# A diffusion-transformer block on one core: x of image 0 in two loads, x*s + x for the first scaling, the scale rows in two parts, another order of the head

## The chip, the cores and the metric

The kernel runs on 1 core of one Trainium2 chip. A core has five engines with a queue of instructions each: TensorE (PE; its weight loads are listed as PEld), VectorE (DVE), ScalarE (ACT), GpSimd (POOL) and SyncE (SP). An engine works through its queue in order and waits on semaphores that other engines, or landed DMAs, raise. DMAs are issued from the queues of SP, ACT and POOL and are moved by 16 DMA engines. The metric is device microseconds of one execution.

## The reference

Two images (B = 2) of N = 256 tokens and D = 1152 features go through one transformer block whose normalised inputs are scaled and shifted by a condition vector c. All data are bfloat16.

```python
mod = (_silu(c) @ w_mod).reshape(B, 6, 1, D)
shift_a, scale_a, gate_a, shift_m, scale_m, gate_m = [mod[:, i] for i in range(6)]
h = _layernorm(x, axis=-1) * (1 + scale_a) + shift_a
qkv = (h @ wqkv).reshape(B, N, 3, H, Dh)          # H = 2 heads, Dh = 576
attn = _softmax(einsum('bqhd,bkhd->bhqk', q, k) * Dh ** (-0.5), axis=-1)
a = einsum('bhqk,bkhd->bqhd', attn, v).reshape(B, N, D) @ wo
x = x + gate_a * a
h2 = _layernorm(x, axis=-1) * (1 + scale_m) + shift_m
return x + gate_m * (_gelu(h2 @ w_fc1) @ w_fc2)   # w_fc1: 1152 x 4608
```

Only the first three lines and the K part of the fourth matter for the change: silu(c), the rows scale_a of w_mod, the layer norm of x, its scaling, and K = h @ (K columns of wqkv). The shift of h is not needed for K here: it adds the same amount to every score of a query, which softmax cancels, so K is made from the scaled input alone ("HK").

## The kernel before

**Planner and queues.** The kernel is written as units of work (`S.unit`, `S.op`), each with an engine, an estimated duration and the regions it reads and writes. From the regions the planner derives the waits. Units of PE and of SP keep the order in which the text gives them. ACT, DVE and POOL are ordered by a list schedule from the estimated durations, except that `S.first` (L940) writes out the order of the head of DVE's and ACT's queues by hand. An engine waits in its queue for whatever the next instruction needs, whatever stands behind it. For a function of ACT the compiler puts the load of the function table ahead of the first instruction that uses it. Where an instruction needs more than one wait, all but the last stand as instructions of their own ahead of it.

**Tiles.** Each image has two token tiles of 128 tokens: tiles t = 0, 1 are image 0, tiles 2, 3 image 1. The feature dimension is cut in nine groups of 128 (kt = 0 to 8). KC = 5 is where the scale columns are cut: groups 0 to 4 are made first, by small matmuls that leave them along partitions ("sca_0" to "sca_8", one for each of nine contraction steps, L849 to L857); groups 5 to 8 come later as rows of two ("scb", L879, 36 matmuls, four for each contraction step).

**Loads (L699 to L713).** ACT issues two: "touch" (L699, 128 pieces of 64 B out of rows spread over w_mod; nothing reads them) and "ld_c" (c). SP issues x of image 0 in one load (`dma(X[:, 0:2, :], xv[0], ...)`, L701, 4608 bytes a partition), x of tile 2 ("ld_x2"), the scale columns of groups 0 to 4 in four loads ("ld_sc0_0" to "ld_sc0_8"), K's weights wk0 and wk1, x of tile 3 ("ld_x3"), wk2 to wk4, the scale columns of groups 5 to 8 in three loads ("ld_sc5_0", "ld_sc5_3", "ld_sc5_6"), wk5 to wk8, and so on.

**The head.** PE first runs matmuls on dummy data ("warm"). It turns c with a transpose ("c_T"). DVE halves it ("c_half", L732), ACT takes tanh ("c_tanh", L733), DVE finishes silu ("c_silu", L734). The statistics of even tiles run on ACT (`ln_stats_act`, L747: a pass of squares "sq", a pass for the mean "sum"; DVE then makes the variance in two small steps, "nvar" and "veps"), those of odd tiles on DVE (`ln_stats_dve`, L738: three "bn", "aggr", "veps"). POOL raises the variance to the power -1/2 ("rstd"). DVE normalises ("xn_t", L763). PE transposes the tile ("xnT_t", L773). For image 0, group 0 is copied from PSUM ("xnT_cp0_0"), 1 is added to the scale columns ("sc1a_0", L807), and each group is multiplied by its column of 1 + s ("hk_kt_b", L812; b is the image). K is then accumulated group by group: `k_pair` (L831) makes two output tiles of 256 columns, and "hk_0_0" opens the first of them.

**Around scb.** After K of image 1's first pair of output tiles (groups 0 to 4, `k_pair((0, 2, 1, 4, 3), 0, 1)`, L878), PE runs the 36 matmuls of scb, and DVE transposes the result ("scb_T", L884), adds 1 ("sc1a_5", L886) and scales groups 5 to 8 of both images, while PE goes on with two more pairs of image 1 for groups 0 to 4. Groups 5 to 8 of K follow. Behind them PE makes the shift rows ("sh"), Q, the scores, V, the output projection and the two MLP matmuls.

Of the kernel before, what the change touches and what calls it, by code (L numbers as in the profile page):

```python
# [493 lines left out]
ALU = mybir.AluOpType  # L494
# [3 lines left out]
P = 128  # L498
NTOK = 512
D = 1152  # L500
KT = 9
# [3 lines left out]
EPS = 1e-5  # L505
# [4 lines left out]
KC = 5  # L510
# [33 lines left out]
def build_kernel(nc, x, c, wqkv, wo, w_mod, w_fc1, w_fc2, out):  # L544
    S = Sched()
# [4 lines left out]
    with (  # L550
# [147 lines left out]

        dma(sb(O_PT, 64)[0:128, :], w_mod.rearrange("(p k) f -> p k f", k=9)[:, 0, D:D + 32], 128 * 64, "touch", eng="act")  # L699
        dma(CSB[0:18, :], c.rearrange("b (k p) -> (b k) p", p=P), 18 * 256, "ld_c", eng="act")  # L700
        dma(X[:, 0:2, :], xv[0], 2 * P * D * 2, "ld_x0")  # L701
        dma(X[:, 2, :], xv[1][:, 0, :], P * D * 2, "ld_x2", run=2304)
        for (ka, kb, cuts) in ((0, KC, (0, 2, 5, 8, 9)), (KC, KT, (0, 3, 6, 9))):
            w = (kb - ka) * P
            for k0, k1 in zip(cuts, cuts[1:]):
                dma(WSC[:, k0:k1, ka * P:kb * P], wmod_v[:, k0:k1, D + ka * P:D + kb * P], (k1 - k0) * P * w * 2,
                    "ld_sc%d_%d" % (ka, k0), run=w * 2)
            for kt in range(ka, kb):
                dma(WK[:, kt, :], wqkv_v[:, kt, D:2 * D], P * D * 2, "ld_wk%d" % kt, run=2304)
                if kt == 1:  # L710
                    dma(X[:, 3, :], xv[1][:, 1, :], P * D * 2, "ld_x3", run=2304)
# [13 lines left out]
        dve(600, lambda e: e.memset(Q4B, 0.0), [], [Q4B], "zq4b")  # L725
        for i in range(7):
            S.unit("pe", 430.0, "warm_a%d" % i)
            mm(ps32(7), IDENT, Q4B, True, True)
# [18 lines left out]
        def ln_stats_act(src, junk, mv_t, msq, rstd_t, tag):  # L747
            mean, var = mv_t[:, 0:1], mv_t[:, 1:2]
            act(1420, lambda e: e.activation(out=junk, in_=src, func=ACTF.Square, scale=D ** -0.5, accum_out=msq), [src], [junk, msq], "sq_" + tag)
            act(1420, lambda e: e.activation(out=junk, in_=src, func=ACTF.Identity, scale=1.0 / D, accum_out=mean), [src], [junk, mean], "sum_" + tag)  # L750
            dve(170, lambda e: e.scalar_tensor_tensor(out=var, in0=mean, scalar=mean, in1=msq, op0=ALU.mult, op1=ALU.subtract),
                [mean, msq], [var], "nvar_" + tag)
            dve(150, lambda e: e.tensor_scalar(out=var, in0=var, scalar1=-1.0, scalar2=EPS, op0=ALU.mult, op1=ALU.add), [var], [var], "veps_" + tag)
            pool(650, lambda e: e.tensor_tensor(out=rstd_t, in0=var, in1=NHALF, op=ALU.pow), [var, NHALF], [rstd_t], "rstd_" + tag)
# [57 lines left out]
        def hk(kt, b, eng="dve"):  # L812
# [3 lines left out]
            if eng == "act":  # L816
# [3 lines left out]
                [src, s1], [dst], "hk_%d_%d" % (kt, b))  # L820

        def k_mm(kts, j, b, bank, half):

# [22 lines left out]

        warm(5, "b")
        for kt in range(0, 2):
            mod_kt(WSC, kt, 0, "sca_%d" % kt, (0, KC))  # L849
        warm(4, "c")  # L850
        xn_T(1)
        for kt in range(2, 5):
            mod_kt(WSC, kt, 0, "sca_%d" % kt, (0, KC))
        xn_T(0)
        warm(2, "d")
        for kt in range(5, 9):
            mod_kt(WSC, kt, 0, "sca_%d" % kt, (0, KC))  # L857
        warm(1, "e")
        xn_T_copy(0, (0,), "dve")
        sc1a(0, KC)  # L860
        for kt in range(KC):
            hk(kt, 0, "act" if kt == 4 else "dve")
        xn_T_copy(0, (8,), "act")
# [14 lines left out]
        k_pair((0, 2, 1, 4, 3), 0, 1)  # L878
        S.unit("pe", KT * 4 * 27.0, "scb")  # L879
        for kt in range(KT):  # L880
            quad_mm(7, WSC[:, kt, :], KC, KT, kt)
        n = 32 * (KT - KC)
        sct, scr = ps32(7, 0, n), MT[:, 0:n]
        dve(c_dve_psum32(n), lambda e: e.transpose(scr, sct), [sct], [scr], "scb_T")  # L884
        scv, sco = scr.rearrange("p (k r) -> p k r", r=32)[:, :, 0:2], SC1A.rearrange("p (k b) -> p k b", b=2)[:, KC:KT, :]
        dve(170, lambda e: e.tensor_scalar(out=sco, in0=scv, scalar1=1.0, scalar2=None, op0=ALU.add), [scv], [sco], "sc1a_%d" % KC)  # L886
        for kt in range(KC, KT):
            for b in range(2):
                hk(kt, b)
        k_pair((0, 2, 1, 4, 3), 1, 1)  # L890
        k_pair((0, 2, 1, 4, 3), 2, 1)
# [34 lines left out]
        for kt in range(KT):  # L926
            for b in range(2):
# [5 lines left out]
                else:  # L933
# [6 lines left out]
        S.first = {  # L940
            "dve": ["zq4b", "bn_ln1_1_0", "c_half", "bn_ln1_1_1", "bn_ln1_1_2", "c_silu", "aggr_ln1_1", "veps_ln1_1", "nvar_ln1_0", "veps_ln1_0",
                    "xn_1", "xn_0", "nvar_ln1_2", "veps_ln1_2", "xnT_cp0_0", "sc1a_0", "hk_0_0", "hk_1_0", "hk_2_0", "hk_3_0", "xn_2",
                    "bn_ln1_3_0", "bn_ln1_3_1", "bn_ln1_3_2", "aggr_ln1_3", "veps_ln1_3", "xn_3", "hk_0_1", "hk_2_1", "hk_4_1", "xnT_cp1_6", "scb_T", "sc1a_5"],
            "act": ["touch", "ld_c", "sq_ln1_0", "c_tanh", "sum_ln1_0", "sq_ln1_2", "sum_ln1_2", "xnT_cp0_8", "xnT_cp0_5", "hk_4_0",
                    "hk_1_1", "hk_3_1", "xnT_cp1_8", "xnT_cp1_5"],
# [362 lines left out]
```

## Time and profile before

| what | us |
|---|---|
| median of 3 runs (244.64 to 244.94) | 244.71 |
| the profiled execution | 245.13 |
| its span | 243.4 |
| PE busy in the span | 237.7 (98%) |
| DVE busy | 116.1 (48%) |
| ACT busy | 67.0 (28%) |
| POOL busy | 22.4 (9%) |
| mean DMA rate over the span | 212 GB/s |

Busy times of a view are sums over instructions; in a timeline each line gives the start in us from the span's beginning, the duration, the engine (a q behind it is its queue: issues and waits), the line of the kernel, the operation, what it writes and reads, how many such instructions the line merges, and in brackets the idle time of the engine before it with what ended that. The profiled execution is one execution; it took 0.42 us more than the median of the runs. Landings of single DMAs are times from the span's start as the trace records them.

### The profile page before, as it was taken

What the parts mean: (1) busy time and instruction counts of PE and PEld (TensorE: products, weight loads), DVE (VectorE), ACT (ScalarE), POOL (GpSimd) and SP (SyncE); (2) the same over time, 40 slices, a digit from 0 to 9 for tenths busy, and PEclk for the clock granted to TensorE, in tenths of its full rate; (3) what the DMA queues carried; (4) which work ended last, traced back from release to release, by engine and by line L of the source; (5) the groups of instructions that cost most, each with busy time, mean ns of one, the idle gap of its engine ahead of it and who ended that gap; (6) DMA issues with size and microseconds to landing.
All of it is one profiled execution on the core that took longest, in us unless ns stands there. A gap on an engine that the chain in (4) does not pass through costs nothing.

```text
span 243.4 us, 3964 instructions
## 1 busy us (share of the span) xinstructions
PE 237.7 (98%) x1700; PEld 145.3 (60%) x1700; DVE 116.1 (48%) x227; ACT 67.0 (28%) x138; POOL 22.4 (9%) x40
## 2 busy tenths in 40 slices
PE   6998999999999999999999999999999999999995
PEld 2587844466667666888644444444556565666664
DVE  2663357888982589769999700000022222111112
ACT  4820340436514206983223332222000000000000
POOL 1300000000023186400000110000000000000000
DMA  6999999999995999969953589100000000000000
GB/s 221 368 375 391 389 386 387 403 413 406 392 350 150 352 389 391 391 201 402 352 166 91 177 294 375 59 0 3 0 16 19 16 16 16 19 16 16 19 28 20
DMA packets 30299, 51.58 MB, mean 212 GB/s; under 512 B 1611, under 2 KB 16971, under 8 KB 30283
## 3 DMA queue, kind: packets, MB, share of 16 engines
q1 hardware_dynamic: 29600, 50.14, 57.6%
q0 software_dynamic: 512, 1.19, 1.5%
q8 instruction: 13, 0.21, 0.4%
q10 hardware_dynamic: 171, 0.01, 0.0%
q14 instruction: 3, 0.02, 0.0%
HBM read 50.15 MB, written 1.19 MB: 211 GB/s over the span
## 4 chain that ended last, share of the span: by engine, by line
PE 91%; DMA 5%; SPq 3%; issue 0%; DVE 0%
PE psum L693 90%; DMA arena<-in_w_mod_dram 5%; SPq L674 3%; PE psum L696 1%; DVE arena L1250 0%; DVE arena L1251 0%
## 5 line engine op out<-in xcount | busy, mean ns | idle before, releaser
L693 PE MATMUL psum<-arena 128*128 128x384 bf16 (+8 forms) x1611 | 234.4, 314 | 2.9 <-POOL arena L719 1.5
L693 PEld LDWEIGHTS psum<-arena 128*128 128x128 bf16 (+2 forms) x1611 | 140.0, 97 | 92.8 <-issue 4.1
L1250 DVE TENSOR_TENSOR arena<-psum,arena 128x384 f32<-128x384 f32 (+2 forms) x13 | 6.9, 527 | 88.8 <-PE psum L693 88.8
L1163 ACT ACTIVATE arena<-psum 128x512 bf16<-128x512 f32 (+1 forms) x45 | 22.8, 511 | 42.4 <-PE psum L693 42.4
L688 ACT ACTIVATE arena<-psum 128x512 bf16<-128x512 f32 (+6 forms) x37 | 18.7, 534 | 36.9 <-PE psum L693 36.6
L1063 DVE SCALAR_TENSOR_TENSOR arena<-arena 128x1152 f32<-128x1152 bf16 x16 | 21.4, 1418 | 0.0
L1034 DVE SCALAR_TENSOR_TENSOR arena<-arena 128x896 f32<-128x896 bf16 x16 | 17.7, 1145 | 0.0
L690 DVE CAST arena<-psum 128x512 bf16<-128x512 f32 (+1 forms) x12 | 7.7, 647 | 11.1 <-PE psum L693 11.0
L674 POOL DMA_DIRECT2D dit_scratch<-arena x6 | 3.6, 605 | 93.6 <-ACT arena L688 54.3
L1129 POOL TENSOR_TENSOR arena<-arena 128x384 f32<-128x384 f32 x12 | 10.9, 912 | 11.2 <-DVE arena L1128 9.1
L741 DVE BATCH_NORM_STATS2 arena<-arena 128x6 f32<-128x384 f32 (+1 forms) x18 | 9.5, 551 | 4.2 <-DMA arena<-in_x_dram 3.5
L1134 ACT ACTIVATE arena<-arena 128x1152 bf16<-128x1152 f32 x4 | 5.4, 1344 | 9.5 <-DVE arena L1133 9.5
L1128 DVE TENSOR_TENSOR arena<-psum,arena 128x384 f32<-128x384 f32 x12 | 6.5, 549 | 2.9 <-PE psum L693 2.8
L696 PE MATMUL psum<-arena 128*128 128x128 bf16 (+1 forms) x89 | 7.1, 219 | 0.4 <-DMA arena<-in_c_dram 0.4
L696 PEld LDWEIGHTS psum<-arena 128*128 128x128 bf16 (+1 forms) x89 | 5.8, 98 | 2.7 <-DMA arena<-in_c_dram 1.3
L1251 DVE TENSOR_TENSOR arena<-arena 128x384 bf16<-128x384 f32 (+2 forms) x13 | 6.9, 527 | 0.5
L1153 ACT ACTIVATE arena<-psum,arena 128x128 bf16<-128x128 bf16 x16 | 6.1, 454 | 3.0 <-PE psum L696 2.2
L1150 DVE TENSOR_SCALAR arena<-psum,arena 128x128 bf16<-128x128 bf16 x20 | 5.5, 338 | 2.9 <-PE psum L696 2.9
L978 ACT ACTIVATE arena<-psum,arena 128x256 bf16<-128x256 f32 x8 | 3.7, 470 | 0.4 <-DVE arena L975 0.3
L745 POOL TENSOR_TENSOR arena<-arena 128x1 f32<-128x1 f32 x6 | 3.3, 553 | 4.8 <-DVE arena L744 4.8
L931 ACT ACTIVATE arena<-arena 128x256 bf16<-128x256 bf16 x6 | 2.5, 494 | 3.3 <-DVE arena L925 3.3
L974 DVE TENSOR_REDUCE arena<-psum 128x2 f32<-128x512 f32 x4 | 2.8, 688 | 0.9 <-PE psum L693 0.9
(57 smaller groups left out, 52.5 us busy)
## 6 DMA issues: line engine op xcount, KB each, us to landing
arena<-in_w_fc_dram SPq DMA_DIRECT2D x9, 1152.0 KB, 7.3
arena<-in_w_fc_dram SPq DMA_DIRECT2D x4, 2592.0 KB, 18.1
arena<-in_w_mod_dram SPq DMA_DIRECT2D x3, 1920.0 KB, 19.6
arena<-in_wqkv_dram SPq DMA_DIRECT2D x18, 288.0 KB, 10.2
arena<-in_w_mod_dram SPq DMA_DIRECT2D x3, 864.0 KB, 13.1
arena<-in_wqkv_dram SPq DMA_DIRECT2D x1, 2592.0 KB, 16.5
arena<-in_wo_dram SPq DMA_DIRECT2D x1, 2592.0 KB, 26.0
arena<-in_w_mod_dram SPq DMA_DIRECT2D x1, 2592.0 KB, 17.9
```

Source lines behind the costliest of these rows:

```text
L674: return S.op(eng, 500.0 if eng == "sp" else 150.0, lambda e: e.dma_start(dst, src), reads=[src], writes=[dst], name=name, dma_bytes=nbyte ...
L688: act(c_act(n), lambda e: e.activation(out=dst, in_=src, func=ACTF.Copy), [src], [dst], name)
L690: dve(c_dve_psum16(n) if psum16 else c_dve_psum32(n), lambda e: e.tensor_copy(dst, src), [src], [dst], name)
L693: S.instr(lambda e: e.matmul(o, lhsT=l, rhs=r, start=st, stop=sp, **kw), reads=[l, r], writes=[o])
L696: S.instr(lambda e: e.transpose(o, i_, idn), reads=[i_, idn], writes=[o])
L741: dve(550, lambda e, s=s, o=o: e.bn_stats(out=o, in_=s), [s], [o], "bn_%s_%d" % (tag, ci))
L1034: dve(150 + FG * 1.1, lambda e, o=o, w=w, s1=s1: e.scalar_tensor_tensor(out=o, in0=w, scalar=s1, in1=o, op0=ALU.mult, op1=ALU.add), [w, s1 ...
L1063: u = dve(1300, lambda e, o=o, w=w, s1=s1: e.scalar_tensor_tensor(out=o, in0=w, scalar=s1, in1=o, op0=ALU.mult, op1=ALU.add), [w, s1, o], ...
L1129: S.op("pool", 930, lambda e, xs=xs, x1c=x1c: e.tensor_tensor(out=x1c, in0=x1c, in1=xs, op=ALU.add), reads=[x1c, xs], writes=[x1c], name=" ...
L1163: act(c_act(ntok), lambda e: e.activation(out=dst, in_=o, func=ACTF.Gelu_apprx_tanh), [o], [dst], "gelu_%d_%d" % (f, tok0))
L1250: dve(c_dve_psum32(w), lambda e, o=o, gm=gm, t1=t1: e.tensor_tensor(out=t1, in0=o, in1=gm, op=ALU.mult), [o, gm], [t1], "fc2_t1_%d_%d" % ( ...
L1251: dve(c_dve_32(w), lambda e, t1=t1, x1c=x1c, ost=ost: e.tensor_tensor(out=ost, in0=t1, in1=x1c, op=ALU.add), [t1, x1c], [ost], "fc2_out_%d ...
```

## The change

It changes six things, all before the shift rows:

1. The load "touch" is taken out, so ld_c is the first on ACT's queue.
2. x of image 0 is loaded in two halves, one for each tile; x of tile 3 is loaded one place earlier, ahead of wk1.
3. The numbers and places of the warm matmuls change (7, 5, 4, 2, 1 become 4, 8, 3, 1, 2), and both transposes xnT_0 and xnT_1 stand side by side, tile 0 first.
4. For group 0 of image 0, and for group 5 of both images, the scaling is done as x*s + x with the raw s ("hk_raw"), ahead of the step that adds 1.
5. scb is cut in two: contraction steps 0 to 5, then six K matmuls, then steps 6 to 8.
6. The order of the head of DVE's and ACT's queues changes: DVE does c_half and c_silu first and xn_0 before xn_1; ACT does c_tanh before sq_0, and takes hk_3_0 over from DVE. In `ln_stats_act`, eps is added to the mean square before the variance is made rather than after.

```diff
-        dma(sb(O_PT, 64)[0:128, :], w_mod.rearrange("(p k) f -> p k f", k=9)[:, 0, D:D + 32], 128 * 64, "touch", eng="act")
         dma(CSB[0:18, :], c.rearrange("b (k p) -> (b k) p", p=P), 18 * 256, "ld_c", eng="act")
-        dma(X[:, 0:2, :], xv[0], 2 * P * D * 2, "ld_x0")
+        for t in range(2):
+            dma(X[:, t, :], xv[0][:, t, :], P * D * 2, "ld_x%d" % t, run=2304)
...
-                if kt == 1:
+                if kt == 0:
                     dma(X[:, 3, :], xv[1][:, 1, :], P * D * 2, "ld_x3", run=2304)
...
-        for i in range(7):
+        for i in range(4):
             S.unit("pe", 430.0, "warm_a%d" % i)
...
-            dve(170, lambda e: e.scalar_tensor_tensor(out=var, in0=mean, scalar=mean, in1=msq, op0=ALU.mult, op1=ALU.subtract),
+            dve(150, lambda e: e.tensor_scalar(out=msq, in0=msq, scalar1=EPS, scalar2=None, op0=ALU.add), [msq], [msq], "veps_" + tag)
+            dve(170, lambda e: e.scalar_tensor_tensor(out=var, in0=mean, scalar=mean, in1=msq, op0=ALU.mult, op1=ALU.subtract, reverse1=True),
                 [mean, msq], [var], "nvar_" + tag)
-            dve(150, lambda e: e.tensor_scalar(out=var, in0=var, scalar1=-1.0, scalar2=EPS, op0=ALU.mult, op1=ALU.add), [var], [var], "veps_" + tag)
...
+        def hk_raw(kt, b, sc):
+            dst, src = HK[:, kt, b * 256:(b + 1) * 256], HX[:, kt, b * 256:(b + 1) * 256]
+            dve(330, lambda e: e.scalar_tensor_tensor(out=dst, in0=src, scalar=sc, in1=src, op0=ALU.mult, op1=ALU.add),
+                [src, sc], [dst], "hk_%d_%d" % (kt, b))
...
-        warm(5, "b")
+        warm(8, "b")
         for kt in range(0, 2):
             mod_kt(WSC, kt, 0, "sca_%d" % kt, (0, KC))
-        warm(4, "c")
+        warm(3, "c")
+        xn_T(0)
         xn_T(1)
         for kt in range(2, 5):
             mod_kt(WSC, kt, 0, "sca_%d" % kt, (0, KC))
-        xn_T(0)
-        warm(2, "d")
+        warm(1, "d")
         for kt in range(5, 9):
             mod_kt(WSC, kt, 0, "sca_%d" % kt, (0, KC))
-        warm(1, "e")
+        warm(2, "e")
         xn_T_copy(0, (0,), "dve")
+        hk_raw(0, 0, ps32(7, 0, 1))
         sc1a(0, KC)
-        for kt in range(KC):
-            hk(kt, 0, "act" if kt == 4 else "dve")
+        for kt in range(1, KC):
+            hk(kt, 0, "act" if kt >= 3 else "dve")
...
-        S.unit("pe", KT * 4 * 27.0, "scb")
-        for kt in range(KT):
+        S.unit("pe", 6 * 4 * 27.0, "scb_0")
+        for kt in range(6):
+            quad_mm(7, WSC[:, kt, :], KC, KT, kt)
+        k_pair((0, 2, 1), 1, 1)
+        S.unit("pe", 3 * 4 * 27.0, "scb_1")
+        for kt in range(6, KT):
             quad_mm(7, WSC[:, kt, :], KC, KT, kt)
...
+        for b in range(2):
+            hk_raw(KC, b, scv[:, 0, b:b + 1])
         dve(170, lambda e: e.tensor_scalar(out=sco, in0=scv, scalar1=1.0, scalar2=None, op0=ALU.add), [scv], [sco], "sc1a_%d" % KC)
-        for kt in range(KC, KT):
+        for kt in range(KC + 1, KT):
             for b in range(2):
                 hk(kt, b)
-        k_pair((0, 2, 1, 4, 3), 1, 1)
+        k_pair((4, 3), 1, 1)
         k_pair((0, 2, 1, 4, 3), 2, 1)
...
-            "dve": ["zq4b", "bn_ln1_1_0", "c_half", "bn_ln1_1_1", "bn_ln1_1_2", "c_silu", "aggr_ln1_1", "veps_ln1_1", "nvar_ln1_0", "veps_ln1_0",
-                    "xn_1", "xn_0", "nvar_ln1_2", "veps_ln1_2", "xnT_cp0_0", "sc1a_0", "hk_0_0", "hk_1_0", "hk_2_0", "hk_3_0", "xn_2",
...
-            "act": ["touch", "ld_c", "sq_ln1_0", "c_tanh", "sum_ln1_0", "sq_ln1_2", "sum_ln1_2", "xnT_cp0_8", "xnT_cp0_5", "hk_4_0",
...
+            "dve": ["zq4b", "c_half", "c_silu", "bn_ln1_1_0", "bn_ln1_1_1", "veps_ln1_0", "bn_ln1_1_2", "nvar_ln1_0", "aggr_ln1_1", "veps_ln1_1",
+                    "xn_0", "xn_1", "veps_ln1_2", "nvar_ln1_2", "xnT_cp0_0", "hk_0_0", "sc1a_0", "hk_1_0", "hk_2_0", "xn_2", "bn_ln1_3_0",
...
+            "act": ["ld_c", "c_tanh", "sq_ln1_0", "sum_ln1_0", "sq_ln1_2", "sum_ln1_2", "xnT_cp0_8", "xnT_cp0_5", "hk_4_0", "hk_3_0",
...
```

## The prediction

> **What bounds the kernel now.** I read the page first. TensorE (PE) is busy for 237.7 of 243.4 us, so only what moves PE's start, or a hole in PE, counts. The chain of work that ended last shows where PE's holes end:
>
> ```profile
> 8.36 11.29 DMA arena<-in_w_mod_dram
> 19.64 0.04 issue
> 19.69 39.98 PE psum L693 x299
> ...
> 109.21 131.75 PE psum L693 x792
> ```
>
> From 19.69 to 240.97 us the chain is PE alone (its one break is 0.07 us at 109.14): whatever PE loses or wins by then, the kernel keeps. What releases PE at 19.69 is a DMA, the last of the scale columns of w_mod, "ld_sc5_6", issued at 8.36 and landed at 19.64. The timeline of PE over the first 21 us shows the holes:
>
> ```profile
> 1.49 3.17 PE L693 MATMUL psum<-arena 128*128 128x512 bf16 x7 [1.49 <-POOL arena L719]
> 5.04 0.19 PE L696 MATMUL psum<-arena 18*128 18x18 bf16 x1 [0.38 <-DMA arena<-in_c_dram]
> ...
> 11.62 1.92 PE L693 MATMUL psum<-arena 128*128 128x256 bf16 x16 [0.53 <-DVE arena L819]
> ...
> 16.57 2.35 PE L693 MATMUL psum<-arena 128*128 128x256 bf16 x38
> 19.69 1.54 PE L693 MATMUL psum<-arena 128*2 128x128 bf16 x22 [0.77 <-DMA arena<-in_w_mod_dram]
> ```
>
> K's matmuls begin at 11.62, after "hk_0_0". The two-row scale matmuls ("scb") begin at 18.41 (trace), run 24 of 36, and stand 0.77 us for that DMA. So the head before 11.62 is not the bound: it could slip by about 0.9 us before the wait at 19.69 would move. The change fills this hole, and so uses up the slack. Third, the timelines of ScalarE (ACT), VectorE (DVE) and GpSimd (POOL), for the chain that leads to 11.62:
>
> ```profile
> 0.79 0.42 ACTq L674 DMA_DIRECT2D arena<-in_w_mod_dram  x1
> 1.24 0.60 ACTq L674 DMA_DIRECT2D arena<-in_c_dram  x1
> 1.88 1.28 ACT L749 ACT_TABLE_LOAD   x1 [1.88 <-issue]
> 4.69 1.16 ACT L749 ACTIVATE arena<-arena 128x1152 bf16<-128x1152 bf16 x1 [1.53 <-DMA arena<-in_x_dram]
> ...
> 5.86 0.17 ACT L733 ACTIVATE arena<-psum 128x18 f32<-128x18 bf16 x1
> 5.98 1.16 ACT L750 ACTIVATE arena<-arena 128x1152 bf16<-128x1152 bf16 x1
> ```
> ```profile
> 5.26 0.18 DVE L732 TENSOR_SCALAR arena<-psum 128x18 f32<-128x18 bf16 x1
> ...
> 7.59 0.57 DVE L763 TENSOR_SCALAR arena<-arena 128x1152 bf16<-128x1152 bf16 x1
> 8.61 0.58 DVE L763 TENSOR_SCALAR arena<-arena 128x1152 bf16<-128x1152 bf16 x1 [0.44 <-POOL arena L754]
> ```
> ```profile
> 6.92 0.57 POOL L745 TENSOR_TENSOR arena<-arena 128x1 f32<-128x1 f32 x1 [0.21 <-DVE arena L744]
> 7.76 0.82 POOL L754 TENSOR_TENSOR arena<-arena 128x1 f32<-128x1 f32 x1 [0.28 <-DVE arena L753]
> ```
>
> The reader is to see two things. ACT loads its function table at 1.88, in 1.28 us, while it has nothing to do (x lands at 4.67). And POOL's power takes 0.57 us alone, 0.82 beside the normalisation xn_1 on DVE.
>
> **Part 1, the hole.** "scb" is cut into 24 and 12 matmuls, with six K matmuls between. Six at 0.109 us (10.4 us busy overlaps; their starts lie 0.109 apart in the trace) are 0.655 us that now stand behind the wait and would stand in it. If scb_0 still began at 18.41, scb_1 would be ready at 18.41 + 1.21 = 19.62 (24 small matmuls 0.34, two changes of shape at 0.1 each, six K matmuls 0.66), just ahead of the DMA. Gain 0.65 us; each 0.1 us that the head slips beyond 0.07 takes 0.1 back. Behind scb, 14 K matmuls (1.53 us) are left to cover the transpose scb_T (0.32) and the first new-form hk_5_0 (under 0.4): covered with about 0.5 us over, and hk_5_1 and the one-op-later sc1a_5 follow in front of matmuls later still.
>
> **Part 2, ACT's order.** The order has c_tanh before sq_0, and touch is gone. In the built program of the changed kernel ACT's queue reads: issue ld_c, wait for DVE's c_half, table load, tanh (waits for PE), Square (waits for x). Before it read: two issues, table load, Square. The load goes with the first function, and c_tanh carries a second wait, for DVE, which stands ahead of the load. So 1.28 us that lay in idle time now lie on this chain: c lands, c_T, c_half, table load, tanh, sq_0.
>
> When does c land? Before, 4.99, behind touch on ACT's queue. Touch's packets moved from 2.58 to 4.31 and it landed at 4.88; c's moved at 3.83 to 4.19 (packet records). With c first, its 18 rows move in touch's place, from about 2.6 to 3.0, and land some 0.7 us later as these two did: 3.7, an estimate. Bounds: c_T cannot start before the four warm matmuls have (1.49 + 4 x 0.427 = 3.2); and if the touch cost c only its 0.45 us of issue, 4.55. I take 3.7 because touch, first in the same queue at the same 0.79, shows it.
>
> Sum: c_T 3.75; c_half 3.98 to 4.15 (5.04 to 5.26 before, and 0.18); load 4.2 to 5.48; tanh 5.50; sq_0 5.63 (0.12 behind tanh's start, as 5.86 to 5.98). Before, 4.69. That x's first half now lands by about 3.9 (the 288 KB load x2 came 0.76 us behind the 576 KB one) wins nothing: sq_0 waits for tanh.
>
> **Part 3, from sq_0 to K.** Both orders need two Act passes, nvar, a power, xn. From sq_2 to nvar_2 took 2.56 (7.14 to 9.70); nvar 0.22; one small DVE step less, since eps is added to msq beforehand; 0.08 to the power; 0.55; xn 0.04 and 0.57. So xn_0 ends at 5.63 + 4.03 = 9.66, its transposes at 10.23. xn_1, formerly finished first (8.17), now stands behind xn_0 on DVE, and its power behind rstd_0 on POOL and beside xn_0: 0.82 instead of 0.55 by the row above. xn_1 runs 9.95 to 10.53. On PE, xnT_1 and all that follows wait for it: transposes to 11.10 (0.51), sca_2 to 4 (0.40), one warm (0.22), sca_5 to 8 (0.53) to 12.25; DVE begins 0.35 later as before (10.72 to 11.07). There the raw form saves its step: before, sc1a 0.17 and a hand-over stood ahead of hk_0_0. The raw operation itself (x*s + x, 256 columns) is not in this trace: between 0.29, hk_0_0's plain form, and 0.38, from L1034's 1145 ns for 896 columns; I take 0.35. K starts at 13.0 against 11.62: 1.38 us late. Cover for the rest of the head: bn_1 (three at 0.55) is held by c_silu until about 5.85 but is done by 7.6, before nvar_0 at 8.2. sca_0 needs ld_sc0_0 (6.64), wk1 lands at about 12.5 now that x3 is ahead of it: both ahead of PE. hk_3_0 on ACT (0.47) is not due for 2.6 us after K starts. From K's start to scb_0 the order is the old one, so the 1.38 us passes through.
>
> **DMA side.** One more SP issue (0.42 us) ahead of all loads is hidden: from ld_sc0_0 on, loads land over 4.9 us after issue, by queueing. Two half loads move 2304-byte packets at about 95 ns instead of 4608 at 178: 0.1 us; touch's 128 packets gone give back up to that. ld_sc5_6 lands at 19.6 to 19.8, scb_1 is ready at 21.0: 1.2 us of cover, and the same cover hides a slower first read of w_mod without touch, priced at nothing (wqkv's first read, not touched before, came 0.74 us behind its forerunner, as its later ones).
>
> **Sum.** 1.38 - 0.07 - 0.655 = +0.66 us. The profiled execution took 245.13 (span 243.4 and 1.73 around it), 0.42 above the median of the runs; I add the difference to the median: 244.71 + 0.66 = 245.4. About 0.2% (0.49 us) can be told from no change.
>
> One rule against it: the Trainium skill, "ScalarE: Activation LUTs", section "What ACT_TABLE_LOAD costs", adds a drain of about 1380 ns to the load's 1283, 2.66 us a switch. The trace agrees on the 1283 (both loads), not on the drain: the load at 99.74 is followed by an ACTIVATE at 101.03, 0.01 us after its end. By the page the sum would be about +2.0 and the time 246.8, an estimate; I go by the row.
>
> **Rivals.**
> *The load stays out of the way* (other side). If ACT still loaded its table before c_half, sq_0 would start at about 4.35, K at 11.7, held by wk1 at 12.5; the hole is filled and the gain stands: 0.6 us, 244.1. For it: the row at 1.88 shows the load needs no data. Against: the queue's order, which ACT has kept in every row. It decides if the load starts before about 3 us. Chance 0.10.
> *The slip just eats the gain.* c lands at 3.2, or the power escapes DVE: 0.5 and 0.27 less, each possible; with both, K at 12.2 and 244.6; with one, 244.9 to 245.1. For it: 0.55 is the power's time alone. Against: both powers now fall where DVE normalises. Chance 0.24.
> *Dearer yet.* (a) ACT stays shut after the first load: the 1.53 us idle after it in the trace does not exclude as much; 246.9. (b) PE's clock. With the head stretched PE stands some 1.5 us for xn_0. Its 512-column matmuls started 0.43 us apart until 6.4 and 0.215 after; if K ran at the slow rate for 3.4 us as at the start, 1.7 more: 247.1. Against (b): holes of 0.53 and 0.77 did not do it. The Trainium skill, "TensorE: Matmul & The Clock Gate", Part 1, has a free-running window of about 3.4 us, and the clock falls after an idle one; by it a 1.5 us hole would not, and the trace has none longer. Chance 0.10 together.
>
> **Numbers.** The forecast 0.56, most of it over the bound of 0.2%. The range, 244.5 to 246.1, leaves out the first rival and the dear ones; c at its late bound, 4.55, would give 246.2. Faster 0.10; same 0.25 (second rival and the forecast's lower edge); slower 0.65.
>
> **What would show it.** In the changed kernel's timelines: the table load at about 4.2 behind c_half, sq_0 near 5.6, POOL's second power about 0.8 us long, K's first matmul near 13.0, no DMA wait left near 19.7 and scb_1 at about 21.0. A table load at 1.5, or K before 12.3, would prove it wrong.

## The result, and the profile after

| | before | after |
|---|---|---|
| median of the runs made together, us | 244.71 (244.34 to 244.94) | 245.41 (245.40 to 246.18) |
| the profiled execution, us | 245.13 | 245.40 |
| its span, us | 243.4 | 243.7 |
| K's first matmul, us from the span's start | 11.62 | 12.66 |
| scb, first to last two-row matmul | 18.41 to 19.81 | 19.43 to 20.75 |

The changed kernel takes 1.0035 times as long (95% interval 1.0024 to 1.0046): 0.3% slower, and the interval lies wholly above 1. Six of its seven runs lie between 245.40 and 245.42; the seventh, 246.18, ran at a mean TensorE clock of 0.993, which an experiment below takes up.

The timelines of the changed kernel, with the columns of those before (start, duration, engine and line, operation, count, idle time and what ended it). First ScalarE:

```profile
0.80 0.60 ACTq L674 DMA_DIRECT2D arena<-in_c_dram  x1
3.80 1.28 ACT L733 ACT_TABLE_LOAD   x1 [3.80 <-DVE arena L732]
5.09 0.19 ACT L733 ACTIVATE arena<-psum 128x18 f32<-128x18 bf16 x1
5.17 1.16 ACT L749 ACTIVATE arena<-arena 128x1152 bf16<-128x1152 bf16 x1
```

The table load now stands behind DVE's c_half (L732) at 3.80, and the squares of tile 0 start at 5.17, though their x landed at 3.63. Then VectorE, and the two powers on POOL:

```profile
8.73 1.23 DVE L763 TENSOR_SCALAR arena<-arena 128x1152 bf16<-128x1152 bf16 x2 [0.35 <-POOL arena L754]
12.02 0.49 DVE L824 SCALAR_TENSOR_TENSOR arena<-arena,psum 128x256 bf16<-128x256 bf16 x1 [1.00 <-PE psum L693]
```
```profile
8.12 0.57 POOL L754 TENSOR_TENSOR arena<-arena 128x1 f32<-128x1 f32 x1 [2.29 <-DVE arena L752]
8.67 0.67 POOL L745 TENSOR_TENSOR arena<-arena 128x1 f32<-128x1 f32 x1
```

Both tiles are normalised from 8.73 to 9.96 (9.19 before, for the later of the two). L824 is the new x*s + x of group 0: 0.49 us. TensorE:

```profile
3.31 0.19 PE L696 MATMUL psum<-arena 18*128 18x18 bf16 x1
3.43 3.57 PE L693 MATMUL psum<-arena 128*128 128x512 bf16 x8
7.42 1.09 PE L693 MATMUL psum<-arena 128*128 128x2 bf16 x13 [0.41 <-DMA arena<-in_w_mod_dram]
9.36 1.33 PE L696 MATMUL psum<-arena 128*128 128x128 bf16 x18 [0.86 <-DVE arena L763]
10.52 1.74 PE L693 MATMUL psum<-arena 128*128 128x2 bf16 x38
12.66 1.91 PE L693 MATMUL psum<-arena 128*128 128x256 bf16 x16 [0.40 <-DVE arena L809]
17.59 5.68 PE L693 MATMUL psum<-arena 128*128 128x256 bf16 x76
```

c is transposed at 3.31, right behind the fourth warm matmul. TensorE then stands 0.41 us for the first scale columns (ld_sc0_0, landed at 7.37) and 0.86 us for the normalised tile. The line at 17.59 runs through scb with no idle time in it: the wait that stood at 19.69 before is gone (the last scale columns landed at 18.60, the second part of scb starts at 20.63). The chain of work that ended last (start, duration, what) has ScalarE, POOL and DVE in it instead of that DMA:

```profile
3.80 1.28 ACT L733
5.08 0.01 issue
5.09 0.19 ACT arena L733
5.28 1.15 ACT arena L749 x2
...
8.73 0.59 DVE arena L763
9.32 0.05 issue
9.36 1.33 PE psum L696 x18
...
12.66 1.91 PE psum L693 x16
```

From the pitch of TensorE's matmuls in the trace (start to start) the profiled executions differ by two terms: K starts 1.035 us later (12.657 against 11.622), and scb, from its first to its last matmul, takes 1.32 us with six K matmuls (0.655) in it, against 1.40 without them. So 1.32 - 0.655 = 0.665 stands against 1.40: 0.73 gained, and 1.035 - 0.73 = +0.30, which is what the profiled executions show (245.40 - 245.13 = +0.27). The median, however, rose by 0.70. What the kernel before usually does is therefore a question of its own, which the second group of experiments takes up.

### The profile page after: what moved, and what is told of

Its sections match the earlier page's. It is cut to its first block, busy times and chain, and to the rows that moved or that the text cites. A ratio compares the mean times of both kernels' runs of the same rounds, so it can differ in the third digit from the quotient of the medians.

```text
span 243.7 us, 3962 instructions
## 1 busy us (share of the span) xinstructions
PE 238.0 (98%) x1699; PEld 144.8 (59%) x1699; DVE 116.9 (48%) x226; ACT 67.5 (28%) x139; POOL 22.3 (9%) x40
## 4 chain that ended last, share of the span: by engine, by line
PE 96%; ACT 2%; DVE 1%; POOL 0%; issue 0%; DVEq 0%; ACTq 0%; POOLq 0%
PE psum L693 93%; PE psum L696 2%; ACT L733 1%; ACT arena L750 1%; ACT arena L749 0%; DVE arena L763 0%; POOL arena L754 0%; DVE arena L824 0%; POOL arena L719 0%; DVE arena L1263 0%; DVE arena L1264 0%; DVE arena L752 0%; POOL arena L718 0%; DVE arena L732 0%; ACT arena L733 0%
## 5 line engine op out<-in xcount | busy, mean ns | idle before, releaser
L693 PE MATMUL psum<-arena 128*128 128x384 bf16 (+9 forms) x1610 | 234.5, 315 | 2.4 <-POOL arena L719 1.5
```

The lines of the kernel that those rows point to most:

```text
L693: S.instr(lambda e: e.matmul(o, lhsT=l, rhs=r, start=st, stop=sp, **kw), reads=[l, r], writes=[o])
```

## Experiments

Theory: the change is slower because the table load has come onto the chain behind c, which makes K 1.03 us late, and what it gains at scb is smaller. Rivals: the lateness is from the scale columns (touch is gone, x comes in two loads), or the gain at scb is whole and something else costs. Twelve further runs were made, two of them of the unchanged kernels; each is compared with runs of the kernel before made on the same chip.

### Is the late table load the cause?

**early_table**: a tiny tanh of a constant ahead of c_tanh; the rest as in the changed kernel.

```diff
+        PRE = sb(misc(4), 4, F32)
+        act(200, lambda e: e.activation(out=PRE, in_=NHALF, func=ACTF.Tanh, scale=0.5), [NHALF], [PRE], "c_pre")
...
-            "act": ["ld_c", "c_tanh", "sq_ln1_0", ...
+            "act": ["ld_c", "c_pre", "c_tanh", "sq_ln1_0", ...
```

> The changed kernel with one tiny tanh of a constant (128x1) ahead of c_tanh on ACT, so that the table load goes with it, right behind the issue of ld_c; nothing of the reference's work is changed. Theory 'table load behind the wait': the load runs at about 1.4 to 2.7, tanh at 3.8, sq_0 at about 3.85 instead of 5.17. K would then start 1.3 us earlier by its own chain (11.35), but the loads hold it: in the changed kernel's trace ld_sc0_8 landed at 10.76 and wk0 at 11.51, wk1 at 12.98, so K starts at 11.6 to 11.9 and its second group not before about 13.05 against 13.54: 0.5 us faster than the changed kernel, 244.9; up to 1.0 (244.4) where these loads land as early as before. Rival 'the other order of DVE and PE costs the time': the load was hidden anyway, K stays at 12.5 or later and the time at 245.3 to 245.5.

**sq_first**: nothing added, only ScalarE's order as before in this place.

```diff
-            "act": ["ld_c", "c_tanh", "sq_ln1_0", "sum_ln1_0", ...
+            "act": ["ld_c", "sq_ln1_0", "c_tanh", "sum_ln1_0", ...
```

> The changed kernel with ScalarE's order as before in one place: the squares of tile 0 ahead of the tanh of c. Nothing added, nothing taken out. Theory (the table load is late because the first function on ScalarE waits for c_half): the load goes to about 1.5, sq_0 starts at 3.65, behind x's first half, 1.5 us earlier than in the changed kernel; the normalised tiles stop being the limit, the scale columns of w_mod (ld_sc0_8, landed at 10.8 to 11.1) become it, and K starts at 11.9 to 12.3: 244.7 to 245.0 at full clock. Rival (the order is not the cause, the two x loads and DVE's new order make K late): K still at 12.6 or later, 245.4.

Measured: early_table 245.05 (ratio 1.0017, interval 1.0000 to 1.0035), sq_first 245.06 (1.0023, 1.0011 to 1.0035), both with executions down to 244.35 and 244.41. ScalarE of early_table, whose load is early too:

```profile
1.41 1.28 ACT L726 ACT_TABLE_LOAD   x1 [1.41 <-PEq L1308]
3.89 1.15 ACT L751 ACTIVATE arena<-arena 128x1152 bf16<-128x1152 bf16 x1
```

Where K starts at full clock early_table's trace can't show, because that execution (246.07) ran at half clock for a stretch. ScalarE and TensorE of sq_first:

```profile
1.43 1.28 ACT L749 ACT_TABLE_LOAD   x1 [1.43 <-PEq L1306]
3.69 1.16 ACT L749 ACTIVATE arena<-arena 128x1152 bf16<-128x1152 bf16 x1 [0.98 <-DMA arena<-in_x_dram]
4.85 0.17 ACT L733 ACTIVATE arena<-psum 128x18 f32<-128x18 bf16 x1
```
```profile
6.81 1.08 PE L693 MATMUL psum<-arena 128*128 128x2 bf16 x13 [0.55 <-DMA arena<-in_w_mod_dram]
8.13 1.33 PE L696 MATMUL psum<-arena 128*128 128x128 bf16 x18 [0.23 <-DVE arena L763]
9.29 1.74 PE L693 MATMUL psum<-arena 128*128 128x2 bf16 x38
11.42 2.14 PE L693 MATMUL psum<-arena 128*128 128x256 bf16 x16 [0.40 <-DVE arena L809]
```

With two names exchanged the load is back at 1.43, squares start when x lands, and K starts at 11.42, earlier than before and 1.23 us earlier than in the changed kernel. So the theory holds: it is the order that makes K late. On the median it is worth less, 245.06 against six runs of the changed kernel at 245.40 to 245.57 on the same chip (after_again, below). This trace is sq_first's fastest execution, and its scale columns landed early (ld_sc0_0 at 6.77, against 7.3 to 8.1 in the other traces of kernels with the new head). That this spread makes its times at full clock, 244.4 to 245.3, is likely but argued: no second trace of sq_first exists. Two limits stand behind the order: the scale columns, and wk1, which comes behind x of tile 3 now. K's second group of matmuls starts 0.346 us after the one ahead of it, at 12.53, instead of 0.109: it waited 0.24 for wk1, landed at 12.40.

### What is the split of scb worth, and how large is the hole?

**before_again**: the kernel before, unchanged. **split_only**: the kernel before with the split alone.

```diff
-        S.unit("pe", KT * 4 * 27.0, "scb")
-        for kt in range(KT):
+        S.unit("pe", 6 * 4 * 27.0, "scb_0")
+        for kt in range(6):
+            quad_mm(7, WSC[:, kt, :], KC, KT, kt)
+        k_pair((0, 2, 1), 1, 1)
+        S.unit("pe", 3 * 4 * 27.0, "scb_1")
+        for kt in range(6, KT):
...
-        k_pair((0, 2, 1, 4, 3), 1, 1)
+        k_pair((4, 3), 1, 1)
```

> The kernel before, unchanged, for a second trace of it. If its spread of 0.6 us comes from the landing of ld_sc5_6, the span of this trace differs from 243.4 by as much as PE's start behind that wait differs from 19.69, and all before and behind stays: at 244.7 us, PE at about 19.3 with a hole of 0.35. If not, PE starts there at 19.7 again and the difference lies outside the span or behind 20 us.

> The kernel before with scb cut in two and the six K matmuls between, nothing else. Theory 'the six matmuls fill the hole': the wait at the last scale load falls from 0.77 to about 0.1 us in a run like the profiled one, and the time by the part of the 0.655 us that the hole has in a usual run. If usual runs of the kernel before are 0.4 us shorter than its profiled execution because that load lands 0.4 us earlier in them, the gain on the median is 0.3 (244.4) and the spread shrinks to 0.1 or so; if the 0.4 us lie elsewhere, the gain is 0.65 (244.06). Rival 'PE loses as much on changes of shape and on the cover behind scb': no gain, 244.6 to 244.8.

**unsplit**: the changed kernel with that part undone.

> The changed kernel with scb in one piece again, everything else left. Theory: the load it could wait for (ld_sc5_6) lands at 18.6 to 18.9, and with the head 1.03 us later the last third of scb is not reached before 19.9, so the split has nothing left to hide: 245.4 as the changed kernel, within 0.1. The prediction's sum by its terms: the slip alone had used the cover up, so also no loss, 245.4. Rival (the split still pays 0.65 us, for another reason than that wait, the scaling of groups 5 to 8 for example): 246.0.

**later_only**: the kernel before with the six K matmuls ahead of scb, which stays in one piece.

```diff
+        k_pair((0, 2, 1), 1, 1)
         S.unit("pe", KT * 4 * 27.0, "scb")
...
-        k_pair((0, 2, 1, 4, 3), 1, 1)
+        k_pair((4, 3), 1, 1)
```

> The kernel before with six K matmuls moved ahead of scb, which stays in one piece. The split puts six K matmuls between its parts and pays for two more changes between large and two-row matmuls, 0.21 us by the traces (20.75 - 19.43 = 1.32 for scb in two parts against 0.455 for scb alone and 0.655 for six K matmuls). Theory (the split costs 0.21 and saves the wait for the last scale columns, which is 0.2 in one trace of the kernel before and 0.97 in the other): with the same delay and no split the fastest runs of before, 244.2, become the rule: 244.2 to 244.4, 0.2 below the split alone (244.48). Rival (the change of shape costs nothing, the split kernel is only noisy): 244.5.

| kernel | median, us | range | ratio to before (95% interval) |
|---|---|---|---|
| before_again | 244.67 | 244.20 to 245.16 | 0.9993 (0.9976 to 1.0011) |
| split_only | 244.48 | 244.37 to 244.84 | 0.9994 (0.9981 to 1.0006) |
| later_only | 244.44 | 244.40 to 246.16 | 1.0000 (0.9985 to 1.0014) |
| unsplit | 245.43 | 245.21 to 246.36 | 1.0044 (1.0027 to 1.0061) |

TensorE of before_again, the same program as the one that the prediction read:

```profile
11.63 1.92 PE L693 MATMUL psum<-arena 128*128 128x256 bf16 x16 [0.52 <-DVE arena L819]
...
16.58 5.66 PE L693 MATMUL psum<-arena 128*128 128x256 bf16 x76
```

The idle 0.77 us at 19.69 is not there: the last line runs on through scb. In the pitch the third part of scb still starts 0.241 us after the matmul ahead of it instead of 0.045, so it waited 0.20; in the first trace that step was 0.985, a wait of 0.94. The load waited for landed at 18.91 here and at 19.64 there. The two profiled executions differ by just this: 245.13 - 244.40 = 0.73, and the waits by 0.94 - 0.20 = 0.74. The wait is thus a matter of the single execution, and the spread of most runs of the kernel before, 244.2 to 245.2, has room for it.

The split is not free either. Uncut, scb takes 0.455 us where nothing waits (unsplit, 19.45 to 19.90); cut, 1.32, of which six K matmuls are 0.655: two more changes between large and two-row matmuls cost 0.21. Unsplit at full clock is indeed 245.21 or 245.22 in three of four executions (245.63 in the fourth) against 245.40: in the changed kernel, whose head is so late that nothing waits at scb, the split costs 0.2 and gains nothing. I had expected 245.4, and it missed by that term. In the kernel before it trades a wait of 0.2 to 0.9 for 0.21: a narrower range, and a median that can't be told from no split.

later_only should then have reached 244.2 and did not. Its trace shows a new wait behind scb, at 21.43, where the K matmuls of groups 5 to 8 begin 0.319 instead of 0.109 after the one ahead. DVE's transpose of scb, which they wait for, in split_only and in later_only:

```profile
20.27 0.32 DVE L888 STREAM_TRANSPOSE arena<-psum 128x128 f32<-128x128 f32 x1 [2.41 <-PE psum L693]
```
```profile
20.52 0.32 DVE L885 STREAM_TRANSPOSE arena<-psum 128x128 f32<-128x128 f32 x1 [2.69 <-PE psum L693]
```

It starts 0.51 us after the last two-row matmul (19.76) where twelve of them stand in a row, and 1.00 us after it (19.52) where 36 do; in unsplit it is 1.00 too (19.90 to 20.90), but there 20 K matmuls cover it and here 14. The split thus also brings the transpose forward. The trace's semaphore events show why. Each matmul raises TensorE's semaphore when it is done, and DVE waits for the last one. The two-row matmuls start 13 ns apart on average but are reported done one by one, 34 ns apart: in later_only the first of the 36 at 19.30, the last at 20.50, and the transpose starts at 20.52. Where a pause lies ahead of the last twelve, the reports catch up in it; after the shorter pause in before_again the transpose starts 0.80 us after the last matmul.

### What do touch and the two x loads do?

**touch_back**: the changed kernel with touch again, behind ld_c. **one_x**: the changed kernel with x of image 0 in one load again.

```diff
+        dma(sb(O_PT, 64)[0:128, :], w_mod.rearrange("(p k) f -> p k f", k=9)[:, 0, D:D + 32], 128 * 64, "touch", eng="act")
...
-            "act": ["ld_c", "c_tanh", ...
+            "act": ["ld_c", "touch", "c_tanh", ...
```
```diff
-        for t in range(2):
-            dma(X[:, t, :], xv[0][:, t, :], P * D * 2, "ld_x%d" % t, run=2304)
+        dma(X[:, 0:2, :], xv[0], 2 * P * D * 2, "ld_x0")
```

> The changed kernel with the small read of spread rows of w_mod put back, behind ld_c on ACT's queue. In the changed kernel's trace the first loads of w_mod landed 0.7 to 0.95 us later than before (ld_sc0_0 7.37 against 6.64, ld_sc0_8 10.76 against 9.81), and PE stood 0.41 us at 7.42 for the first. Theory 'hidden': the head waits for x's statistics (xn_0 from 8.73) and not for these loads; they land earlier again, the wait at 7.42 goes, and the time stays at 245.4, within 0.1. Rival 'the touch was worth its place': K starts earlier and the time falls by 0.3 us or more.

> The changed kernel with x of image 0 in one load again, everything else left. Theory (the two x loads win nothing, since the squares of tile 0 wait for the tanh until 5.17 and x in one load lands at 4.7, and they push the scale columns back): K at 12.66 and 245.4 as the changed kernel at full clock, and the first scale columns (ld_sc0_0) land at 6.6 to 6.9 as in the kernel before, against 6.8 to 8.1 in the traces of kernels with two x loads; TensorE then stands for the normalised tile alone, some 1.3 us from about 8.0 on, so executions at a lower clock may still be seen. Rival (the missing or later touch pushes the scale columns back, not x): ld_sc0_0 still at 7.4 or later, and the stand at the scale columns stays.

At full clock both are the changed kernel, to the hundredth: 245.40 to 245.42 and 245.42 to 245.44. So neither part is worth anything in time: x in one load lands at 4.33 and the squares wait for the tanh until 5.17. But each also has executions that lie higher, seven of ten and three of nine (medians 246.4, ratio 1.0078 with interval 1.0053 to 1.0103; and 245.43, 1.0037, 1.0022 to 1.0051), which is the next question.

TensorE of one_x:

```profile
7.37 1.08 PE L693 MATMUL psum<-arena 128*128 128x2 bf16 x13 [0.92 <-DMA arena<-in_w_mod_dram]
9.36 2.10 PE L696 MATMUL psum<-arena 128*128 128x128 bf16 x18 [0.91 <-DVE arena L762]
```

The first scale columns still land at 7.32, so it is not the two loads alone that push them back; with touch behind c it was 7.42, against the expectation that they would land earlier again. They landed at 6.6 to 6.9 in the kernels with touch ahead of c and x in one load (before, before_again, split_only, later_only), and otherwise only in sq_first's one trace. The packets of that load usually take 55 ns; the slowest of its first ones took 0.5 to 0.8 us in those four, 0.9 in best (touch ahead of c, x in two loads, below), 1.0 to 1.8 us in the kernels with touch behind c or without it, and 0.4 in sq_first. Undoing either part alone doesn't bring the columns back, and what it takes is not settled.

### Why do some executions take 0.7 to 2.4 us more?

In them the mean clock that TensorE was granted is about 0.993 or 0.986 instead of 1.000. **after_again** is the changed kernel once more; **keep_warm** gives TensorE three more warm matmuls ahead of the scale columns.

```diff
-        warm(8, "b")
+        warm(11, "b")
```

> The changed kernel as it is, once more, beside the others. Theory (the head slips by 1.03 us and nothing else differs): runs at full TensorE clock at 245.4, with hardly any spread, K's first matmul at 12.66. The kernel with touch put back had seven of ten runs 0.7 to 2.2 us above that, at a mean clock of 0.993 or 0.986. If this comes from the changed head (TensorE stands 0.41 and 0.86 us in it) and not from touch, this kernel shows such runs too, in more than a third of them; if touch makes it, hardly any, as in the first set (one of seven).

> The changed kernel with three more warm matmuls (0.65 us) where TensorE waits for the first scale columns. Theory (the executions at a lower mean clock come from that wait: where the columns land late, TensorE stands about 1.3 us there and then runs at half rate for one or two stretches of 3.41 us): the stand shrinks to at most 0.7 us, the executions near 247.6 disappear, those near 246.2 become rare, and the others stay at 245.4, since the normalised tile still comes later than the warm matmuls end. Rival (the low clock has nothing to do with TensorE's standing): a third or more of the executions above 246 as with the changed kernel in this chip's last set.

after_again: six runs at 245.40 to 245.57, three at 247.56 to 247.79 (median 245.44, ratio 1.0059, interval 1.0034 to 1.0084). keep_warm: 11 runs at 245.41 to 245.71 and none above (245.44; 1.0034, 1.0024 to 1.0043). The profiled execution of after_again was one of the three. TensorE there, and its windows between 6.65 and 20.30 (window, length, busy time and count of PE, PEld, DVE, ACT, POOL, granted clock, DMA share, GB/s):

```profile
8.18 1.08 PE L693 MATMUL psum<-arena 128*128 128x2 bf16 x13 [1.28 <-DMA arena<-in_w_mod_dram]
9.37 1.79 PE L696 MATMUL psum<-arena 128*128 128x128 bf16 x18
```
```profile
6.65:10.06 3.41, 2.02 (x24) 1.02 (x24) 2.17 (x7) 3.38 (x6) 1.22 (x2) 1.00 1.03 367
10.06:13.47 3.41, 3.41 (x48) 2.26 (x49) 1.24 (x5) 1.33 (x4) 0.55 (x1) 0.50 1.03 399
13.47:16.89 3.42, 3.42 (x18) 2.46 (x17) 2.72 (x8) 0.79 (x2) 0.55 (x1) 0.50 1.09 363
16.89:20.30 3.41, 3.41 (x42) 3.16 (x40) 0.69 (x2) 0.11 (x1) 0.00 (x0) 1.00 1.07 383
```

The columns landed at 8.13, TensorE stood 1.28 us, and in the stretch of 3.41 us that holds this stand it was busy for 2.02. In the two stretches after it the clock is 0.50, and K's 256-column matmuls start 0.214 us apart instead of 0.109. The other two traces with a drop had 1.71 us (early_table, one stretch) and 1.79 us (one_x, two) of busy time in the stretch ahead of it; the traces that stayed at full clock had 2.36 (best, below), 2.41 (keep_warm), 2.64 (sq_first) and more in each stretch of the head, as far as the record shows where the stretches lie (in ten of the fourteen traces). The phase of these stretches differs from one execution to the next, so how much of the head's idle time falls into one is a matter of chance. Over all runs, 16 of 41 executions of the changed head (the changed kernel, touch_back, one_x, unsplit) lay above 245.9, and none of the 11 of keep_warm, which has the same head but for 0.65 us of dummy work. The kernel before has 5 of 118, all on one chip, and one of these five at a mean clock of 1.000; of the other kernels early_table has 3 of 12, sq_first 2 of 12, best 1 of 12, later_only 1 of 11, split_only and early_touch_x3 none of 11. The counts alone would not settle it, since keep_warm and the kernels of the 41 ran on different chips, but on keep_warm's chip later_only and best did have such an execution. That idle time of TensorE in the head starts the drop is what the traces and the counts agree on; how little busy time it takes lies between 2.02 and 2.36 us here, and why the drop lasts one stretch or two is open.

### A version that beats both?

**early_touch_x3**: early_table with touch behind ld_c and x of tile 3 behind wk1 again. **best**: touch ahead of ld_c, ScalarE's order sq_0, sum_0, c_tanh, DVE's first statistics ahead of silu, warm matmuls 7 and 5, x of tile 3 behind wk1, and scb in one piece behind the six K matmuls.

```diff
-            "act": ["ld_c", "c_tanh", "sq_ln1_0", "sum_ln1_0", ...
+            "act": ["touch", "ld_c", "sq_ln1_0", "sum_ln1_0", "c_tanh", ...
-            "dve": ["zq4b", "c_half", "c_silu", "bn_ln1_1_0", "bn_ln1_1_1", "veps_ln1_0", "bn_ln1_1_2", "nvar_ln1_0", ...
+            "dve": ["zq4b", "bn_ln1_1_0", "c_half", "bn_ln1_1_1", "veps_ln1_0", "bn_ln1_1_2", "nvar_ln1_0", "c_silu", ...
```

> The changed kernel with a tiny tanh of a constant ahead of the tanh of c (the table is loaded at once), with touch put back behind c's load, and with x of tile 3 behind wk1 again: an attempt to keep the changed kernel's parts and lose its late head. Theory: the scale columns of w_mod set the end of the head (ld_sc0_8 landed at 10.5 with touch, 10.8 without); K at 11.6 to 11.9, 244.4 to 244.7 at full clock, level with the kernel before. If wk1 had held K's second group in the kernel with the early table alone, this one starts it 0.7 us sooner. If touch raises the share of runs at a lower clock, it shows here too.

> An attempt to beat both: the changed kernel with touch ahead of c's load again, squares and mean of tile 0 ahead of the tanh, DVE's first statistics ahead of silu, x of tile 3 behind wk1, warm matmuls 7 and 5, and scb in one piece behind the six K matmuls. Theory: with touch first the scale columns land as before (ld_sc0_0 at 6.7, ld_sc0_8 at 9.9) although x comes in two loads; the normalised tile is ready at 7.9; K at 11.1 to 11.4 against 11.63 before: 243.8 to 244.1. Rival (the two x loads themselves push the scale columns back, whatever touch does): ld_sc0_0 at 7.4 or later, ld_sc0_8 at 10.6, K at 11.9 to 12.2 and 244.4 to 244.7.

early_touch_x3 244.52 (244.13 to 245.00; ratio 1.0001, interval 0.9992 to 1.0010), best 244.56 (244.24 to 245.93; 1.0003, 0.9990 to 1.0017): both as the kernel before, neither better. early_touch_x3 is 0.54 below sq_first on the same chip; it differs from it by the early table, touch and the place of x of tile 3, and which of these counts is not separated. TensorE of early_touch_x3, and of best:

```profile
7.55 1.09 PE L693 MATMUL psum<-arena 128*128 128x2 bf16 x13 [0.52 <-DMA arena<-in_w_mod_dram]
...
10.70 1.19 PE L693 MATMUL psum<-arena 128*128 128x2 bf16 x22 [0.44 <-DMA arena<-in_w_mod_dram]
12.20 1.91 PE L693 MATMUL psum<-arena 128*128 128x256 bf16 x16 [0.32 <-DVE arena L812]
```
```profile
7.39 1.08 PE L693 MATMUL psum<-arena 128*128 128x2 bf16 x13 [1.05 <-DMA arena<-in_w_mod_dram]
...
11.45 1.91 PE L693 MATMUL psum<-arena 128*128 128x256 bf16 x16 [0.36 <-DVE arena L810]
...
19.83 1.43 PE L693 MATMUL psum<-arena 128*2 128x128 bf16 x21 [0.44 <-DMA arena<-in_w_mod_dram]
```

In the first the scale columns hold TensorE twice (at 7.55 for ld_sc0_0 and at 10.70 for ld_sc0_5), and K starts at 12.20, where 11.6 to 11.9 was expected. In the second K does start at 11.45, 0.17 earlier than before, but the last scale columns landed at 19.78 in this execution (18.61 in later_only's), and TensorE stands for them at scb: 0.44 us by the idle time, 0.61 by the pitch (0.657 instead of 0.045). What the head gains is lost again there. With touch ahead of c the first columns still landed at 7.35 and ld_sc0_8 at 10.31, close to what the rival of best's expectation has; K came earlier than the rival has it, but the time, 244.56, is the rival's and not the theory's.

## Why the prediction was right, and where only its sum was

The forecast was 245.4 in a range of 244.5 to 246.1; measured 245.41, slower by 0.3%. The mechanism is the predicted one: the table load behind c_half makes K late, and the split gives back a part. Its terms are not right: two errors of 0.3 to 0.4 us cancel, so that the number fits to 0.01 us is luck.

**Part 2, the order of ScalarE: right in kind, 0.46 too late.** The load came behind c_half as predicted, 1.28 us long. The term that was mis-sized is c's landing: 3.7 was taken from touch's packets, but c's 18 rows moved from 1.77 to 2.23 and had landed at 2.53, so c_T started right behind the four warm matmuls, at 3.31, near the lower of the two bounds (3.2). So load 3.80 for 4.2, squares 5.17 for 5.63. That the prediction weighed the drain of the Trainium skill, "ScalarE: Activation LUTs", section "What ACT_TABLE_LOAD costs" (about 1380 ns behind a load of 1283), against the row was right: here too the load takes 1.28, and the tanh follows 0.01 us after its end (3.80 + 1.28 = 5.08, 5.09).

**Part 3, from the squares to K.** To the end of xn_0: 4.03 predicted, 4.14 measured (5.17 to 9.31). POOL's second power does take longer beside DVE, 0.67 and not 0.82, so xn_1 ends 0.65 behind xn_0 instead of 0.87. The step on the raw form failed: it was to take 0.40 from DVE's start to K, against 0.55 for "add 1, then scale" (11.07 to 11.62). It took 0.64 (12.02 to 12.66). The operation itself took 0.49, outside the bounds of 0.29 to 0.38 and just as long as adding 1 and scaling one after the other (11.07 to 11.57), so x*s + x saves nothing here. The other 0.09 is TensorE's. K's first matmul waits for DVE and for the weights wk0, which had long landed (11.51). In the trace the wait for DVE is now the one that stands ahead as an instruction of its own (12.55, 0.05 long, behind hk_0_0's end at 12.51); before, that was the wait for wk0, and it was over at 10.68. (The bracket of the row at 12.66 names sc1a_0, L809, but the wait for DVE was met at 12.55, before sc1a_0 ended at 12.59.) In all: -0.46 + 0.11 - 0.22 + 0.24 = -0.33, and K at 12.66 for 13.0. The slip is 1.04, not 1.38.

**Part 1, the hole.** In the profiled execution the split and the slip gained 0.73, as predicted (0.07 + 0.655), and scb_1 began 1.20 us after scb_0, where 1.21 was predicted. It is the same as the wait, 0.94 in the pitch (the idle time shows 0.77), less the 0.21 of two more changes of shape: the prediction's sum holds these changes in the time to scb_1, and its 0.07 is what they leave.

**The sum: the step that failed** is "I add the difference to the median". Of the wait that the change fills, 0.94 us were in that one execution, which was slow for this very reason, and 0.20 in another of the same kernel. Against its own execution the sum should have read 245.13 + 0.66 = 245.79, and 245.40 was measured. Against the other execution the terms measured here give 244.40 - 0.20 + 1.04 + 0.21 = 245.45. That is near where the changed kernel stands at full clock, with hardly any spread, since nothing in it waits for that DMA any more. On the median the change costs 0.70, so the usual run gains 0.34 at scb and not 0.73. A slip 0.34 too long and a gain 0.39 too large for the usual run made 245.4.

**DMA side.** Touch's removal was "priced at nothing" with the 1.2 us at scb for cover. The cover is there, but the scale columns of groups 0 to 4 are due at the head first: in the two traces of the changed kernel the first of them landed 0.7 and 1.5 us later than before, and TensorE waited for them for 0.41 and 1.28 us. At full clock this costs nothing, as the normalised tile comes later still: K starts at 12.65 to 12.67 in the changed kernel, touch_back, unsplit and keep_warm, though ld_sc0_0 landed anywhere from 7.37 to 7.80.

**The rivals.** "The load stays out of the way" did not happen. early_table and sq_first make it happen, and give 245.05 and 245.06, not 244.1. sq_first's one trace is the rival's picture, K at 11.42 and its second group held by wk1 until 12.53, but that execution took 244.41 and is its fastest; in early_touch_x3's trace it is the scale columns that hold the head, which the rival did not price. "The slip just eats the gain" had half its condition, c at its early bound; the raw form took half of that back. Of "dearer yet", (a) is refuted by the load's row. (b), TensorE's clock falling back, was held unlikely for holes of up to 1.5 us, and it happens, in 4 of 16 executions of the changed kernel, at 246.2 to 247.8 where 247.1 was worked out. Its "3.4 us as at the start" is not in the trace that it was read from, where the matmuls of 512 columns start 0.43 us apart from 1.49 to 6.42, though 3.41 us is the length of the stretches that the drops showed later. The stretch ahead of a drop holds the stand for the scale columns, which the prediction did not have, and in one_x a part of the one for the normalised tile. The Trainium skill, "TensorE: Matmul & The Clock Gate", Part 1, has the clock fall after an idle window of about 3.4 us; by it a stand of 1.3 us should do nothing. The length agrees with the trace (3.413 us), the condition does not: stretches that were idle for 41 to 50% were enough.

## What to carry to other kernels

Look which instruction of ScalarE comes first with a function, and what it waits for: the table load stands behind that wait, so the first function should be one whose input is there early, or needs none. Before a hole is priced at what one profile shows, look at a second execution and at the spread of the times: a wait for a DMA can be 0.2 us in one and 0.9 in the next, and the sum must be made against the execution that has it. Where a head waits for loads, dummy matmuls can fill the wait: here they cost nothing, and none of the 11 executions with them lost clock.

## What the hardware showed beyond that

- TensorE's clock fell to half after a stretch of 3.41 us in which it was busy for 1.71 to 2.02 us, in three traces, and did not after one with 2.36 us or more. A half-rate stretch costs 0.7 to 1.3 us here, two of them 2.1 to 2.4.
- Two-row matmuls between large ones: two more changes of shape cost 0.21 us. They start 13 ns apart but are reported done 34 ns apart, so an engine that waits for the last of 36 in a row starts 1.00 us after it, and 0.51 after the last of 12.
- x*s + x on 256 bfloat16 columns takes 0.49 us with its scalar in PSUM and 0.48 with it in SBUF (two in a row start 0.40 apart), against 0.29 for x*s (0.20 apart).
- With touch ahead of c and x in one load the first scale columns land at 6.6 to 6.9; in every other arrangement tried, but for sq_first's one trace (6.77), at 7.3 to 8.1.
